# Causal masks as products in row groups, one transpose piece for rows 0 to 255, and a new order in a fused attention, experts and gated convolution kernel

## The chip, the cores and the metric

One core of a Trainium2 chip runs the whole program. The metric is the device time of one execution in microseconds; the time of a kernel is the median of its runs. The engines are TensorE (PE), VectorE (DVE), ScalarE (ACT), GpSimd (POOL) and SyncE (SP), which issues all DMAs here.

## The reference

Three layers follow one another, for 4 batch elements of 576 rows and 512 features.

```python
# 1 attention, 8 heads of 64: averaged over groups of 4 rows, plus a band |i-j| < 4
out_d   = softmax(scale * q_d @ k_d.T) @ v_d            # 144 x 144, repeated 4 times
out_loc = softmax(where(|i-j| < 4, scale * q @ k.T, -1e9)) @ v
x = out_d_repeated + out_loc
# 2 experts, 4 of them, each causal attention of 64 features; the 2 best by gate count
for e in range(4):
    s = scale * (x @ wq[e]) @ (x @ wk[e]).T
    s = where(causal, -1e9, s)                          # causal: key after query
    out += weight_e[:, None] * (softmax(s) @ (x @ wv[e]) @ wo[e])
# 3 gated convolution with 5 taps over rows
result = (sigmoid(conv5(out)) * (out @ w_val)) @ w_out
```

## The kernel before

Features lie on the partitions, rows in the columns. Most products are done as three float32r products of split operands (`mm3`, lines 1126 to 1128: high by high, low by high, high by low). The 576 rows of a batch element are taken in halves of 256 and 320 columns.

**Pieces and planner.** The program is registered as pieces: each has an engine, a cost, the buffers that it reads and writes, and a function that issues its instructions. `Plan.order` then walks simulated time with these costs and picks, engine by engine, the ready piece with the lowest due number whose buffers are free. The due numbers are a list written out in the kernel (`DUE`, one for each piece), and the engine of a piece that could run on several is a digit of another list (`PICK`). The order that comes out is the program's; at run time every engine works through its own queue in it.

**Attention** (`load_pair`, `down_path`, `band_scores`, `band_values`) runs for 4 pairs of heads of each batch element. SP loads queries, keys and values of a pair; pairs of rows are added (lines 891 and 898), the averaged scores are line 1000, the band scores line 1053 after a mask product of line 1045, the softmax lies on DVE, ACT and POOL (lines 940 to 987), its transposes are lines 1010 and 1066, the values lines 1026 and 1085, and the split result is x (lines 744 and 761).

**Projections** (`project`) turn x into values and gate logits (line 1192) and queries and keys (line 1210), each as four accumulated `mm3` products, the weights split at the start. The product of two weight matrices is line 842.

**Experts** (`experts`) come in two halves: query blocks T = 0 and 1 (rows 0 to 255), then T = 2, 3 and 4; `pr` is a pair of experts, one on partitions 0 to 63 and one on 64 to 127. `expert_scores` does the score products of both experts in row groups of 64 (line 1266) and then adds the causal mask to the diagonal block as one full-array product of an identity and `cmask` for each T and expert (line 1270). `exponentials` takes the minimum (line 1292, DVE) and the exponential (line 1300, ACT). `keys_on_rows` transposes the exponentials into two PSUM banks, one for each half of the query rows (line 1323), and copies each bank to SBUF (line 736, DVE or ACT). The weighted sum with the values is line 1426; `factors` brings the sums and gates to rows (lines 1358 to 1394); line 1432 multiplies both.

**Gated convolution** (`tail`): the product with `wo`, the taps as lines 1472 to 1486, the gate, the product with `w_val` and the last one with `w_out`, and the result's DMA (line 1524).

The next batch element's attention is registered between the experts and the tail of this one, so that their pieces can fill each other's waits.

Of the kernel before, what the change touches and what calls it, by code (L numbers as in the profile page):

```python
# [14 lines left out]
BF16 = mybir.dt.bfloat16  # L15
# [12 lines left out]
    "c_d": 5, "c_mo": 8, "c_ms": 3, "c_mt": 6, "c_o": 4, "c_s": 3, "c_t": 4, "c_w": 3, "o_00": 0, "o_01": 1,  # L28
# [255 lines left out]
class Plan:  # L284
# [64 lines left out]
    def order(self):  # L349
# [37 lines left out]
        while True:  # L387
            for e, queue in queues.items():
# [38 lines left out]
                if e == "pe":  # L427
                    if p.kind != groups:
                        cost += 0.09 if p.kind else 0.14
                        groups = p.kind  # L430
# [54 lines left out]
def f32r(n):  # L485
    return max(0.459 * n + 5, 112) / 1000
# [1097 lines left out]
```

## Time and profile before

| | us |
|---|---|
| median of 3 runs | 410.54 (410.47 to 414.11) |
| profiled execution, its own time | 409.69 |
| its span, first to last instruction | 408.0 |
| TensorE busy | 370.2 |
| VectorE busy | 317.6 |
| ScalarE busy | 253.2 |
| GpSimd busy | 192.0 |

The span is 1.7 us shorter than the profiled execution's own time, which is 0.85 us under the median of the runs. Busy times are sums over the span, and matmuls overlap in the array, so a busy TensorE need not be at its peak. The mean granted clock of TensorE is 0.937 of full speed.

### The profile page before, as it was taken

The page shows a single profiled execution, that of the slowest core. Times are in us where ns is not written, and L with a number is a line of the kernel's source. Part 1 is how long each engine was busy: PE and PEld are TensorE (multiplying, and loading weights), DVE is VectorE, ACT ScalarE, POOL GpSimd, SP SyncE. Part 2 cuts the span into 40 slices and gives each one's busy share as a digit, 9 for nine tenths or more (in the row PEclk, how much of TensorE's full clock was granted, in tenths as well). Part 3 has the DMA queues.
Part 4 walks back from the last instruction along what each step waited for, and adds up shares of the span by engine and source line. Part 5 has one row for each costly group of instructions (what it writes and reads, how often), then busy time and mean ns, then how long its engine had stood idle before and what let it go on. Part 6 is the DMA issues. An engine that isn't in the chain of part 4 may idle for free.

```text
span 408.0 us, 12119 instructions
## 1 busy us (share of the span) xinstructions
PE 370.2 (91%) x4672; PEld 317.0 (78%) x4672; DVE 317.6 (78%) x893; ACT 253.2 (62%) x879; POOL 192.0 (47%) x273
## 2 busy tenths in 40 slices
PE   1755779998888989999999999999999999999996
PEld 1444368886667777997988899988997799988896
DVE  3899579579779998799889499498977665958771
ACT  3477354377946975866648687365777456368571
POOL 7495365046537563825427357034654135224260
PEclk9965568999589999999999999999999999999999
DMA  7982445214202431421131244102120000001012
GB/s 217 247 258 65 144 123 158 67 38 124 77 31 71 103 108 38 137 73 42 42 108 41 74 134 123 55 6 69 45 91 16 2 2 2 0 34 35 2 39 79
DMA packets 26122, 31.81 MB, mean 78 GB/s; under 512 B 2384, under 2 KB 17872, under 8 KB 26064
## 3 DMA queue, kind: packets, MB, share of 16 engines
q1 hardware_dynamic: 26064, 31.03, 26.2%
q8 instruction: 37, 0.61, 0.6%
q14 instruction: 21, 0.17, 0.2%
HBM read 26.31 MB, written 4.72 MB: 76 GB/s over the span
## 4 chain that ended last, share of the span: by engine, by line
PE 66%; DVE 17%; DMA 6%; ACT 5%; issue 2%; POOL 2%; SPq 1%; ACTq 0%; POOLq 0%; DVEq 0%
PE ps L1126 14%; PE ps L1127 13%; PE ps L1128 13%; PE ps L1426 4%; PE ps L1266 3%; PE ps L1323 3%; DMA vw<-in_vx_dram 2%; PE ps L1026 2%; PE ps L1085 2%; PE ps L842 2%; PE ps L1000 2%; DMA kt<-in_kT_dram 1%; PE ps L1053 1%; ACT p L949 1%; PE ps L1066 1%
## 5 line engine op out<-in xcount | busy, mean ns | idle before, releaser
L1486 DVE SCALAR_TENSOR_TENSOR row<-ps,cw,row 128x256 f32<-128x256 f32 (+1 forms) x89 | 43.4, 509 | 7.6 <-ACT row L1472 2.7
L1300 ACT ACTIVATE pe<-ps,mmin 128x128 f32<-128x128 f32 (+4 forms) x80 | 41.5, 524 | 11.0 <-DVE mmin L1292 5.9
L949 ACT ACTIVATE p<-ps,mx 128x54 f32<-128x54 f32 (+1 forms) x120 | 40.4, 337 | 11.2 <-PE ps L1066 3.7
L1484 POOL TENSOR_TENSOR row<-row,row 128x320 f32<-128x320 f32 (+1 forms) x39 | 32.5, 841 | 23.4 <-DVE row L1486 8.7
L1292 DVE TENSOR_REDUCE mmin<-ps 128x1 f32<-128x512 f32 (+4 forms) x80 | 35.8, 474 | 7.6 <-PE ps L1270 6.6
L1126 PE MATMUL ps<-gh,wout_h 128*128 128x256 f32 (+1 forms) x128 | 39.5, 308 | 2.3 <-DVE qb L1236 1.3
L1126 PE MATMUL ps<-xh,wqk_h 128*128 128x256 f32 (+1 forms) x128 | 40.2, 314 | 0.9 <-DVE kl L761 0.9
L1128 PE MATMUL ps<-gh,wout_l 128*128 128x256 f32 (+1 forms) x128 | 37.9, 296 | 0.0
L1127 PE MATMUL ps<-gl,wout_h 128*128 128x256 f32 (+1 forms) x128 | 37.8, 295 | 0.0
L1127 PE MATMUL ps<-xl,wqk_h 128*128 128x256 f32 (+1 forms) x128 | 37.7, 295 | 0.0
L1128 PE MATMUL ps<-xh,wqk_l 128*128 128x256 f32 (+1 forms) x128 | 37.7, 295 | 0.0
L987 POOL TENSOR_TENSOR p<-p,sm 128x324 f32<-128x324 f32 (+1 forms) x29 | 23.1, 800 | 16.9 <-DVE sm L976 8.7
L1426 PE MATMUL ps<-mpT,vE 128*64 128x320 f32 (+4 forms) x224 | 27.8, 381 | 0.0
L1000 PE MATMUL ps<-kd,qd 64*64 64x144 f32 x192 | 19.0, 337 | 9.7 <-POOL kd L898 8.8
L1126 PEld LDWEIGHTS ps<-gh,wout_h 128*128 128x128 f32 x128 | 24.2, 189 | 3.5 <-DVE qb L1236 1.6
L1126 PEld LDWEIGHTS ps<-xh,wqk_h 128*128 128x128 f32 x128 | 24.1, 188 | 2.6 <-DVE kl L761 1.1
L1127 PEld LDWEIGHTS ps<-xl,wqk_h 128*128 128x128 f32 x128 | 24.2, 189 | 0.2 <-issue 0.2
L1128 PEld LDWEIGHTS ps<-gh,wout_l 128*128 128x128 f32 x128 | 24.1, 188 | 0.1
L1127 PEld LDWEIGHTS ps<-gl,wout_h 128*128 128x128 f32 x128 | 24.1, 189 | 0.0
L1126 PE MATMUL ps<-wvg_h,xh 128*128 128x260 f32 (+1 forms) x80 | 23.8, 297 | 0.4 <-DVE row L1432 0.4
L1128 PEld LDWEIGHTS ps<-xh,wqk_l 128*128 128x128 f32 x128 | 24.1, 188 | 0.0
L1426 PEld LDWEIGHTS ps<-mpT,vE 128*64 128x64 f32 (+1 forms) x224 | 14.6, 141 | 12.1 <-issue 3.9
(225 smaller groups left out, 1230.0 us busy)
## 6 DMA issues: line engine op xcount, KB each, us to landing
vw<-in_vx_dram SPq DMA_DIRECT2D x32, 162.0 KB
qt<-in_qT_dram SPq DMA_DIRECT2D x16, 288.0 KB
kt<-in_kT_dram SPq DMA_DIRECT2D x16, 288.0 KB
v<-in_vx_dram SPq DMA_DIRECT2D x16, 288.0 KB
out_dram<-o SPq DMA_DIRECT2D x16, 160.0 KB
v<-in_w_val_dram SPq DMA_DIRECT2D x4, 512.0 KB
v<-in_w_out_dram SPq DMA_DIRECT2D x4, 512.0 KB
out_dram<-o SPq DMA_DIRECT2D x16, 128.0 KB
```

The costliest lines, as they stand in the source:

```text
L949: nc.scalar.activation(pv()[:, i], sv()[:, i], AF.Exp, scale=scale, bias=mx.t[:n, i:i + 1], accum_out=sums()[:, i:i + 1])
L987: ENG[norm].tensor_mul(pv(), pv(), sm.t[:n, :g].unsqueeze(2).to_broadcast([n, g, w]))
L1000: nc.tensor.matmul(s.t[r, t * SD:(t + 1) * SD], qd.t[r, t, :], kd.t[r, :], start=True, stop=True)
L1126: nc.tensor.matmul(p, ah, bh, start=first, stop=False)
L1127: nc.tensor.matmul(p, ah, bl, start=False, stop=False)
L1128: nc.tensor.matmul(p, al, bh, start=False, stop=last)
L1266: nc.tensor.matmul(s.t[:, o:o + P * (t + 1)], a.t[r, P * t:P * t + P], z.t[r, :P * (t + 1)], start=(k == 0 and t == T[0]), stop=False)
L1292: nc.vector.tensor_reduce(out=m.t[:, a:a + 1], in_=s.t[:, o:o + n], op=ALU.min, axis=AX.X)
L1300: nc.scalar.activation(pe.t[:, c0:c1], s.t[:, o:o + c1 - c0], AF.Exp, bias=m.t[:, 0:1], scale=-1.0, accum_out=sums.t[:, a:a + 1] if last e ...
L1426: nc.tensor.matmul(av.t[64 * e:64 * e + 64, z:n], vE.t[:kr, j, 2 * pr + e, :], pT.t[:kr, e, k0:k0 + n - z], start=(j == 0), stop=(j == Tl))
L1484: nc.gpsimd.tensor_add(g.t[:, :nn], g.t[:, :nn], g2.t[:, :nn])
L1486: nc.vector.scalar_tensor_tensor(g.t[:, :nn], x2.t[:, k:k + nn], cw.t[:, m, k:k + 1], g.t[:, :nn], op0=ALU.mult, op1=ALU.add)
```

## The change

1. **Masks.** The mask of a block T was one full-array product for each expert, 128 columns. It becomes two products in row groups of 64 for each expert: rows 0 to 63 of the query block get the triangle and 64 columns of the large value (128 columns in all), rows 64 to 127 the triangle over the last 64 columns. The two experts use different row groups, and a copy of the identity with its column halves exchanged (`identx`) serves where row group and output half differ. 64 mask products become 128. The constants `cmask` and `cmask2` become one tile `causal`; `identx` is two more small copies.
2. **Rows 0 to 255.** The exponentials of T = 0 and T = 1 are written into one tile for each expert (T = 1 behind column 128) and not two. Their transposes were a piece of 4 and a piece of 8 with two PSUM banks and two copies each (128 and 256 columns); they become one piece of 12 with two banks and two copies of 384 columns. In all 8 transpose pieces and 16 copies fewer, and the same number of transposes.
3. **Order and engines.** All due numbers and engine digits are new, and so are two caps on PSUM banks: `c_d` from 5 to 6, `c_s` from 3 to 4. The planner's costs are changed at some twenty places (the issue of a DMA, float32r products, GpSimd, and others); they touch nothing but the order.

```diff
 PARAMS = {
-    "c_d": 5, "c_mo": 8, "c_ms": 3, "c_mt": 6, "c_o": 4, "c_s": 3, "c_t": 4, "c_w": 3, "o_00": 0, "o_01": 1,
+    "c_d": 6, "c_mo": 8, "c_ms": 3, "c_mt": 6, "c_o": 4, "c_s": 4, "c_t": 4, "c_w": 3, "o_00": 0, "o_01": 1,
...
 def f32r(n):
-    return max(0.459 * n + 5, 112) / 1000
+    return max(0.4533 * n + 2.4, 112) / 1000
...
+            nc.vector.tensor_copy(identx[:, 0:64], ident[:, 64:128])
+            nc.vector.tensor_copy(identx[:, 64:128], ident[:, 0:64])
...
-            nc.gpsimd.memset(cmask, 0.0)
-            nc.gpsimd.affine_select(out=cmask, in_=cmask, compare_op=ALU.is_ge, fill=BIG, base=0,
-                                    pattern=[[-1, P]], channel_multiplier=1)
-            nc.gpsimd.memset(cmask2, 0.0)
+            nc.gpsimd.memset(causal[:, 0:64], 0.0)
+            nc.gpsimd.memset(causal[:, 64:P], BIG)
...
                 for t, o in zip(T, at):
-                    for s in ss:
-                        nc.tensor.matmul(s.t[:, o + P * t:o + P * t + P], identb, cmask, start=False, stop=(t == T[-1]))
+                    for u, d in enumerate((o + P * t, o + P * t + 64)):
+                        for e, s in enumerate(ss):
+                            r = slice(64 * e, 64 * e + 64)
+                            nc.tensor.matmul(s.t[:, d:o + P * t + P], (identb if u == e else identx)[r], causal[r, 0:P - 64 * u],
+                                             start=False, stop=(t == T[-1] and u == 1))
...
+            if Ts == (0, 1):
+                blocks, c, w, o = (2, 0, 1), 0, P, 0
+            else:
+                blocks, o = tuple(range(T, -1, -1)), off
+                c = base - T * w
+                if c < 0:
+                    c, o = c + off, 0
+            nf, pts = len(blocks), [bank("mt"), bank("mt")]
+
+            @piece("pe", 0.066 * 2 * nf, pes, pts + [(pT, "%dt" % T)], kind="row")
+            def _():
+                for e, pe in enumerate(pes):
+                    for k, j in enumerate(blocks):
+                        for u, pt in enumerate(pts):
+                            r, i = slice(64 * u, 64 * u + 64), (nf * e + k) * 64
+                            nc.tensor.transpose(pt.t[:, i:i + 64], pe.t[r, j * P:(j + 1) * P], ident[r, r])
...
-                    pes = {}
+                    pes = [buf("pe") for _ in range(2 if Ts[0] < NTOK - 1 else 1)]
                     for T, e, sp in expert_scores(y, pr, Ts):
-                        pes.setdefault(T, []).append(exponentials(T, e, sp, es if T == NTOK - 1 else rs))
-                    for T in Ts:
-                        keys_on_rows(b, pr, T, pes[T], pT, base, w, P * (T - T0))
+                        exponentials(T, e, sp, es if T == NTOK - 1 else rs, pes[e], P if Ts == (0, 1) and T else 0)
+                    keys_on_rows(b, pr, Ts, pes, pT, base, w, P * (Ts[-1] - T0))
```

What the two lists of due numbers say, put in ascending order, of TensorE's pieces around the first experts (batch element 0, `pr` = 0, from their scores of T = 0 and 1 to the transposes of these):

```
old: scores pr0 T0,1 | 5 attention pieces of element 1 (lines 1053, 1066, 1026, 1000, 1085), scores pr1 T0,1 | transposes T0
new: scores pr0 T0,1 | 12 query and key products of element 0's second half (columns 256 to 575), 7 attention pieces
     of element 1, scores pr1 T0,1, scores pr0 T2 | transposes T0,1
```

In the old list those 12 products all stand before the first scores. By the same reading the piece behind a masked score piece is, in the new list, one in row groups 14 times of 24 (lines 1010, 1066 and 1323), one in another division of the array 7 times and a full-array one 3 times. SP's first loads, by the same reading: old, queries of pair 0 (288 KB), part of `w_val` (512 KB), keys of pair 0 (288 KB); new, part of `wqk` (256 KB), part of `w_val` (512 KB), keys of pair 0 (288 KB), part of `wo` transposed (128 KB), queries of pair 0 (288 KB). Of the 129 digits that place work of element 0's attention and of the query, key, value and `w_val` weights, 57 name DVE in the old list and 44 in the new one, 29 and 36 ACT, 38 and 44 POOL; 5 and 5 name a form without that step.

## Rows read from the trace of the kernel before

**Rows 1.** The page, parts 1 and 2: TensorE's line, and the clock in 40 slices.

```profile
PE 370.2 (91%) x4672; PEld 317.0 (78%) x4672; DVE 317.6 (78%) x893; ACT 253.2 (62%) x879; POOL 192.0 (47%) x273
...
PEclk9965568999589999999999999999999999999999
```

**Rows 2.** Windows by stage: length, busy us of each engine (instructions), granted clock, DMA share, GB/s.

```profile
0.00:8.80 8.80, 0.00 (x0) 0.00 (x0) 2.35 (x12) 3.79 (x10) 7.16 (x33) 1.00 0.75 224
8.80:23.70 14.90, 11.48 (x213) 7.55 (x214) 12.96 (x34) 7.61 (x35) 7.56 (x9) 1.00 0.92 239
23.70:57.70 34.00, 24.12 (x379) 17.59 (x378) 26.42 (x65) 19.77 (x81) 20.21 (x29) 0.50 0.49 141
57.70:64.70 7.00, 5.04 (x122) 4.03 (x120) 6.43 (x18) 5.39 (x24) 4.22 (x5) 0.75 0.58 179
64.70:100.00 35.30, 34.40 (x435) 29.68 (x436) 27.76 (x82) 18.79 (x74) 14.81 (x19) 1.00 0.32 87
100.00:102.10 2.10, 0.54 (x21) 0.31 (x12) 2.00 (x9) 1.87 (x10) 0.86 (x3) 1.00 0.18 42
102.10:115.80 13.70, 12.50 (x84) 8.93 (x84) 9.42 (x33) 9.12 (x42) 5.42 (x9) 0.50 0.19 57
115.80:194.00 78.20, 71.75 (x892) 61.36 (x891) 71.48 (x190) 55.39 (x188) 44.25 (x53) 1.00 0.27 79
194.00:398.00 204.00, 203.59 (x2510) 181.07 (x2507) 157.50 (x455) 129.69 (x419) 86.68 (x119) 1.00 0.15 46
398.00:408.00 10.00, 6.75 (x46) 6.44 (x44) 1.25 (x3) 1.77 (x4) 0.86 (x1) 1.00 0.21 75
```

**Rows 3.** TensorE's timeline, 92 to 107: start, length, instruction, idle before and its releaser.

```profile
91.92 0.31 PE L1127 MATMUL ps<-xl,wqk_h 128*128 128x320 f32 x1
...
92.50 0.31 PE L1128 MATMUL ps<-xh,wqk_l 128*128 128x320 f32 x1
...
93.96 0.47 PE L1266 MATMUL ps<-kh,qh 64*128 64x128 f32 x4
...
99.32 0.91 PE L1085 MATMUL ps<-pT,vw 54*64 54x48 f32 x48
101.79 0.34 PE L1323 MATMUL ps<-ident,pe 64*128 64x64 f32 x4 [1.56 <-DVE row L1101]
103.06 0.69 PE L1323 MATMUL ps<-ident,pe 64*128 64x64 f32 x8 [0.93 <-DVE mpT L736]
```

**Rows 4.** Windows, 2 to 8 us: the rate of the first loads.

```profile
2.00:8.00 6.00, 0.00 (x0) 0.00 (x0) 1.93 (x6) 1.79 (x7) 5.26 (x24) 1.00 0.91 292
```

**Rows 5.** TensorE's timeline, 271 to 274: masks of T = 0 and 1, then transposes.

```profile
272.08 0.45 PE L1266 MATMUL ps<-kl,qh 64*128 64x128 f32 x4
272.31 0.45 PE L1266 MATMUL ps<-kh,ql 64*128 64x128 f32 x4
272.68 0.40 PE L1270 MATMUL ps<-cmask,identb 128*128 128x128 bf16 x4
273.01 0.46 PE L1323 MATMUL ps<-ident,pe 64*128 64x64 f32 x8
273.40 0.83 PE L1000 MATMUL ps<-kd,qd 64*64 64x144 f32 x10
```

**Rows 6.** TensorE's timeline, 337 to 339.2: masks followed by a full-array product.

```profile
338.12 0.39 PE L1266 MATMUL ps<-kh,ql 64*128 64x128 f32 x4
338.44 0.40 PE L1270 MATMUL ps<-cmask,identb 128*128 128x128 bf16 x4
338.65 0.37 PE L1126 MATMUL ps<-wvg_h,xh 128*128 128x260 f32 x1
```

**Rows 7.** Groups by line and shape, DVE: the copies of transposed exponentials (busy, mean ns).

```profile
L736 DVE COPY mpT<-ps 128x384 f32<-128x384 f32 x7 | 3.8, 551 | 0.9 <-PE ps L1323 0.9
...
L736 DVE COPY mpT<-ps 128x256 f32<-128x256 f32 x8 | 3.3, 417 | 0.3 <-PE ps L1323 0.2
...
L736 DVE COPY mpT<-ps 128x128 f32<-128x128 f32 x8 | 2.2, 276 | 0.0
```

More of the change, by code (lines that the diff above doesn't have):

```diff
@@ L428, in order @@
                     if p.kind != groups:
-                        cost += 0.09 if p.kind else 0.14
+                        cost += 0.1
                         groups = p.kind
@@ L497, in gps @@
 def gps(n, k=1):
-    return 0.15 * k + 0.0021 * n + 0.08 * (k - 1)
+    return 0.13 + 0.00185 * n
 def moved(rows, size, queues=16):
@@ L678, in late_constants @@
     def late_constants():
-        @piece("dve", 0.15, [], [late], after=[eye], kind="port")
+        @piece("dve", 0.4, [], [late], after=[eye], kind="port")
         def _():
             nc.vector.tensor_tensor(fold, ident[:, 0:64], ident[:, 64:128], op=ALU.add)
+            nc.vector.tensor_copy(identx[:, 0:64], ident[:, 64:128])
+            nc.vector.tensor_copy(identx[:, 64:128], ident[:, 0:64])
         @piece("pool", 2.0, [], [late])
         def _():
-            nc.gpsimd.memset(cmask, 0.0)
-            nc.gpsimd.affine_select(out=cmask, in_=cmask, compare_op=ALU.is_ge, fill=BIG, base=0,
-                                    pattern=[[-1, P]], channel_multiplier=1)
-            nc.gpsimd.memset(cmask2, 0.0)
+            nc.gpsimd.memset(causal[:, 0:64], 0.0)
+            nc.gpsimd.memset(causal[:, 64:P], BIG)
             for h in range(2):
-                m = cmask2[64 * h:64 * h + 64, :]
+                m = causal[64 * h:64 * h + 64, 0:64]
                 nc.gpsimd.affine_select(out=m, in_=m, compare_op=ALU.is_ge, fill=BIG, base=0,
@@ L729, in cost, with whole @@
         return vec(n, k, k - 1) if eng == "dve" else gps(n, k)
+    def whole(eng, n, src):
+        return 0.13 + 0.0009 * n if eng == "pool" else cost(eng, n, src)
     def copy(eng, n, out, src, reads, writes):
@@ L740, in split @@
         eh = pick(name + "h", "act", "dve", "pool") if inside else pick(name + "h", "act", "dve")
-        @piece(eh, cost(eh, n, read), [read], [wh], kind=port(eh) if inside else None)
+        @piece(eh, whole(eh, n, read), [read], [wh], kind=port(eh) if inside else None)
         def _(src=src):
@@ L775, in chunk @@
         if src.dtype != mybir.dt.int64:
-            @piece("sp", 0.65, [], [f], delay=moved(P, 4 * n), kind="dma")
+            @piece("sp", 0.5, [], [f], delay=moved(P, 4 * n), kind="dma")
             def _():
@@ L787, in part @@
             return (a0, a1)[k].t[:, :n].bitcast(I32)
-        @piece("sp", 0.65, [], [raw], delay=moved(P, 8 * n), kind="dma")
+        @piece("sp", 0.5, [], [raw], delay=moved(P, 8 * n), kind="dma")
         def _():
@@ L794, in whole @@
             return f.t[:, :n].bitcast(I32)
-        @piece("act", act(n, True), [raw], [a1])
+        @piece("act", act(n, True) + 0.03, [raw], [a1])
         def _():
@@ L861, in load_pair @@
         qt, kt, v4, vw = buf("qt"), buf("kt"), buf("v4"), buf("vw")
-        @piece("sp", 0.65, [], [qt], delay=moved(P, 4 * S), kind="dma")
+        @piece("sp", 0.5, [], [qt], delay=moved(P, 4 * S), kind="dma")
         def _():
             nc.sync.dma_start(out=qt.t, in_=qT[b, hp])
-        @piece("sp", 0.65, [], [kt], delay=moved(P, 4 * S), after=ends, kind="dma")
+        @piece("sp", 0.5, [], [kt], delay=moved(P, 4 * S), after=ends, kind="dma")
         def _():
             nc.sync.dma_start(out=kt.t[:, KB], in_=kT[b, hp])
-        @piece("sp", 0.65, [], [v4], delay=moved(144, 2048, 12), kind="dma")
+        @piece("sp", 0.5, [], [v4], delay=moved(144, 2048, 12), kind="dma")
         def _():
@@ L876, in load_pair @@
         for h in range(NR):
-            @piece("sp", 0.65, [], [vw], delay=moved(WK * 2 * NC, 4 * P), kind="dma")
+            @piece("sp", 0.5, [], [vw], delay=moved(WK * 2 * NC, 4 * P), kind="dma")
             def _(h=h):
@@ L978, in softmax @@
         norm = pick("n_" + key, "act", "dve", "pool")
-        @piece(norm, g * (act(w, True) + 0.09) if norm == "act" else cost(norm, g * w) - 0.08 * (norm == "pool"),
+        @piece(norm, g * (act(w, True) + 0.09) if norm == "act" else cost(norm, g * w),
                [p, sm], [p], kind=port(norm))
@@ L993, in down_path @@
         s = bank("s")
-        @piece("pe", 0.735, [qd, kd], [s], kind="quad")
+        @piece("pe", 0.66, [qd, kd], [s], kind="quad")
         def _():
@@ L1038, in band_scores @@
         ss = [bank("s"), bank("s")]
-        @piece("pe", 1.0, [qt, kt], ss, after=[edges, eyeb], kind="quad")
+        @piece("pe", 0.74, [qt, kt], ss, after=[edges, eyeb], kind="quad")
         def _():
@@ L1058, in band_values @@
         vw, pTs, pts = ld[2], [buf("pT"), buf("pT")], [bank("t"), bank("t")]
-        @piece("pe", 0.36, ps, pts, after=down + blanks, kind="row")
+        @piece("pe", 0.41, ps, pts, after=down + blanks, kind="row")
         def _():
@@ L1075, in band_values @@
         pos = [bank("o"), bank("o")]
-        @piece("pe", 0.62, [vw] + pTs, pos, after=down, kind="quad")
+        @piece("pe", 0.735, [vw] + pTs, pos, after=down, kind="quad")
         def _():
@@ L1133, in gates @@
         sh = [P, NTOK, E, E]
-        @piece("dve", 1.9, [L], [ge, gw, gm], kind="port")
+        @piece("dve", 1.63, [L], [ge, gw, gm], kind="port")
         def _():
@@ L1152, in _ @@
             nc.scalar.activation(gw.t[:, 0], gw.t[:, 0], AF.Exp)
-        @piece("dve", 1.2, [gw, gm], [gw, gm], kind="port")
+        @piece("dve", 0.95, [gw, gm], [gw, gm], kind="port")
         def _():
@@ L1256, in expert_scores @@
             at = [sum(P * (u + 1) for u in T[:k]) for k in range(len(T))]
-            @piece("pe", sum(3 * f32r(P * (t + 1)) + 0.16 for t in T), [(qh, (mine,)), (ql, (mine,)), (kh, half), (kl, half)], ss,
+            @piece("pe", sum(3 * f32r(P * (t + 1)) + 0.15 for t in T), [(qh, (mine,)), (ql, (mine,)), (kh, half), (kl, half)], ss,
                    kind="row")
@@ L1280, in _, with exponentials @@
                 if c1 == S:
-                    nc.tensor.matmul(s.t[:, h - 64:h], identb, cmask2, start=False, stop=True)
+                    nc.tensor.matmul(s.t[:, h - 64:h], identb, causal[:, 0:64], start=False, stop=True)
             sp.append((s, 0, c0, c1))
         return [(T[0], 0, sp)]
-    def exponentials(T, e, sp, sums):
+    def exponentials(T, e, sp, sums, pe, off):
         last = T == NTOK - 1
-        pe, m = buf("pe"), buf("mmin")
+        m = buf("mmin")
         for a, (s, o, c0, c1) in enumerate(sp):
@@ L1312, in place @@
             return pT.t[:, :, c:c + nf * w].rearrange("p e (j q) -> p e j q", q=w)[:, :, :, a:a + n]
-        if T < NTOK - 1:
-            pts = [bank("mt"), bank("mt")]
-            @piece("pe", 0.058 * 2 * nf, pes, pts + [(pT, "%dt" % T)], kind="row")
-            def _():
-                for e, pe in enumerate(pes):
-                    for j in range(nf):
-                        for u, pt in enumerate(pts):
-                            r, i = slice(64 * u, 64 * u + 64), (nf * e + nf - 1 - j) * 64
-                            nc.tensor.transpose(pt.t[:, i:i + 64], pe.t[r, j * P:(j + 1) * P], ident[r, r])
-            for u, pt in enumerate(pts):
-                copy(pick("mp_%d%d%d%d" % (b, pr, T, u), "act", "dve"), P * nf, lambda u=u: place(o + 64 * u, 64),
-                     lambda pt=pt: pt.t[:, :nf * P].rearrange("p (e j q) -> p e j q", e=2, q=64), [pt], [(pT, "%d%d" % (T, u))])
-            return
         pe, pt, pt2 = pes[0], bank("mt"), bank("mt")
@@ L1520, in _ @@
                 nc.vector.tensor_scalar_mul(o.t[:, :nn], p.t[:, :nn], 0.5)
-        @piece("sp", 0.65, [o], [], delay=moved(P, 4 * nn), kind="dma")
+        @piece("sp", 0.5, [o], [], delay=moved(P, 4 * nn), kind="dma")
         def _():
```

40 lines of the change are left out of this document (23 added, 17 removed), and 416 rows, old and new, of the table DUE.

## Prediction

> **What bounds the kernel now.** I read the page's first two parts, then windows cut where the clock or TensorE's load changes, then TensorE's timeline at the one place in the middle where it stands still, and last the timelines around the masks. TensorE is busy 91% of the span [rows 1], and the windows show that this is two regimes [rows 2]. From 194 to 398 us it is busy 203.59 of 204.00 us at full clock: there only less TensorE work makes the kernel shorter. Before 194 it waits, and the clock falls. In the first 8.8 us it does nothing. From 8.8 to 64.7 it is idle for 14.9 - 11.48 = 3.4, 34.0 - 24.12 = 9.9 and 7.0 - 5.04 = 2.0 us, with the clock at half (1.2 GHz, 0.50 in the column) from 23.7 to 57.7 and for half of the next 7 us. VectorE is busy there for 12.96 + 26.42 + 6.43 = 45.8 of 55.9 us, more than the other two elementwise engines. A second fall is at 102.1 to 115.8. In between and after it are small holes: 0.9 us in 64.7 to 100, 6.45 in 115.8 to 194. What an edit is worth is therefore a question of where its work stands.
>
> **The stall at 100 us, the largest term.** The scores of the first pair of experts start at 93.96, their first transposes at 101.79 and the second ones at 103.06 [rows 3]: minimum, exponential and their queues take 7.8 and 9.1 us. TensorE's other work ends with the band values that start at 99.32, and it waits 1.56 and 0.93 us. After this wait the clock is at half until 115.8. The loss in numbers [rows 2]: 2.10 - 0.54 = 1.6 us idle, 13.70 - 12.50 = 1.2 us idle, and 12.50 us of busy time at half clock of which half, 6.25 us, would not have been needed. Sum 9.0. In the new order twelve query and key products stand between these scores and the transposes. Each is three matmuls of 320 columns that start (92.50 - 91.92) / 4 = 0.145 us apart [rows 3], so 12 x 3 x 0.145 = 5.2 us. The scores and the pieces that filled the gap before took 99.32 + 0.91 - 93.96 = 6.3 us, and they are all still there. 11.5 us of work against a chain of 9.1 us (the later of the two, since one piece now waits for all four exponentials): covered, with 2.4 us to spare. Behind the transposes of T = 0 nothing waits that the wait for T = 1 could hold up, because the weighted sum needs both. I take the whole 9.0; the range of this term is 0 to 9.0. Next late after it is the chain from the transposes over their copies, the weighted sum and line 1432 to the tail; the new list also places products of the next batch element there.
>
> **The head.** Against the change: in the new order the queries of pair 0 come behind 256 + 512 + 288 + 128 KB, so that both operands are there after 1472 KB and not after 1088. At the 292 GB/s of the first loads [rows 4] the 384 KB are 1.3 us, at a place where TensorE and the engines behind it have nothing else. For it: 13 of 57 pieces leave VectorE for ScalarE and GpSimd in this part. At the 0.42 us of a 256-column operation [rows 7] that is 5.4 of its 45.8 busy us; VectorE is busy for 82% of the stretch, so not all of it comes back, and I take 60%, 3.3 us. Sum -2. Bounds: +2 (the loads come late and VectorE was not what was waited for) and -7 (all 5.4, and 1.6 more since some of the half-clock work meets a full clock).
>
> **Small holes.** 7.4 us are idle in 64.7 to 100 and 115.8 to 194 at full clock [rows 2]. VectorE is busy for 71.48 of 78.2 us in the second stretch, so an order cannot fill all of it. With 16 PSUM copies fewer, each pair of copies of 128 and 256 columns becoming one of 384, VectorE or ScalarE wins 276 + 417 - 551 = 142 ns each time [rows 7], 2.3 us in all and 0 in the saturated part, where it is hidden beside TensorE. I take -5, between 0 and -7.4.
>
> **The masks on TensorE.** Four full-array masks (T = 0 and 1, two experts) take 338.65 - 338.44 = 0.21 us [rows 6], 53 ns each, 0.107 a T. In row groups the two experts can run side by side: 128 + 64 columns, at best 0.08 a T. The nearest row for what they do in row groups is the transposes, also with 64 rows of weights, 128 columns of them and few moving columns: 8 in 273.40 - 273.01 = 0.39 us [rows 5], 49 ns each, so four take 0.196. Stream: -0.027 to +0.089 a T, times 32 blocks -0.9 to +2.8. Then the changes of the array's division. Low-by-high scores take 0.23 when the same division follows (272.08 to 272.31) and 0.37 when the masks follow (272.31 to 272.68), so 0.14 is the change; the masks there take 0.33 until the transposes, against 0.21 where a full-array product follows: another 0.12 [rows 5, 6]. A piece followed by another in row groups saves both, one followed by a full-array product saves none, since the change only moves behind the masks. 24 pieces: 0 to -6.2, together -7.1 to +2.8. In the new list 14 of the 24 are followed by a piece in row groups, 7 by one in another division (which save the first change only) and 3 by a full-array one: 14 x 0.26 + 7 x 0.14 = 4.6 us, against the middle of the stream's range, +0.95. I take -3.5.
>
> The Trainium skill speaks against this part: "TensorE: Matmul & The Clock Gate", section "LDWEIGHTS (loading the stationary operand)", says that a weight load takes its time by the columns of the weights, not by the rows. By that, 64-row loads are as long as the old ones and there are twice as many, so that the stream stands at its worse end: +2.8 - 4.6 = -1.8 in place of -3.5, and the whole sum 1.7 us higher. No row of before shows 64-row bf16 loads.
>
> **The merged transposes** are the same 12 instructions; 8 pieces fewer save at most 8 x 0.14 us of division changes [rows 5]. I take -0.5.
>
> **The sum.** Stall -9, head -2, holes -5, masks -3.5, transposes -0.5: -20 from the profiled 409.7 gives 389.7. The median of the runs is 0.85 above the profiled execution, so 390.5. The edits proper are worth 4 of this; the rest is the order.
>
> **Rivals.**
> *The wait moves.* VectorE is 91% busy in 115.8 to 194 [rows 2]; if it delivers late there, what is gained at 100 us is in part given back as new waits without a fall of the clock. Half of the stall (4.5), half of the holes (2.5), and 4 of edits: -11, 399.5. For it: VectorE keeps almost as much work. Against it: the twelve products stand where the wait was.
> *The head leaves the half clock early.* If the rebalanced pieces keep TensorE fed from about 43 us on, 14 of the 34 half-clock us, with 14/34 x 24.12 = 9.9 us of busy time, would run at full clock: 5.0 less, and 3 of the idle time with it, 382.5. For it: a work shift away from VectorE. Against it: 9.9 us of idle time in 34.
> *The order doesn't do on the chip what its list says.* The planner's costs are not the chip's; the old order too was planned without the stall that it shows. If a comparable stall comes back, the holes stay and the head is no better, only the edits' 4 us or less remain: 406.5 to 411.
> *Slower: the merged transposes stop the queue.* TensorE works its queue in order, and the merged piece waits for four exponentials, which came 1.27 us after the first two [rows 3]. Where fillers run out, TensorE stands still as at 100 us. One such place cost 9.0. [...] If it happens for both pairs of element 0 and one of element 1, 27 us are lost where 9 were, less 11 of the other terms: about 418. Against it: after 194 us the list has no lack of fillers.
>
> Not a rival, but a bound: after 194 us nothing but TensorE work counts, so a gain over 28 us would need most of the head's losses too.
>
> **Chances.** Forecast 0.55, the wait moves 0.20, the head at full clock 0.12, no effect 0.08, slower 0.05. A measurement of this kernel tells about 1% from no change, 4.1 us. Faster by more: 0.55 + 0.20 + 0.12 = 0.87; within: 0.08; slower: 0.05. The range should hold the forecast, the wait that moves and most of the early full clock: 381 (the early full clock, with 1.5 more of the masks' better end) to 404 (the wait that moves, with the masks at -1.8 and 2.8 more of the head's worse end).
>
> **What will show it.** Right: between the first scores and transposes of the experts TensorE has no idle time, and the clock has one half-clock stretch in the head and none around 100 us; the saturated stretch begins some 16 us earlier; the masks of T = 0 and 1 start 0.23 us after the last scores and not 0.37. Wrong would make it: a second fall of the clock anywhere behind the head, a first averaged-scores product later than 11 us, or VectorE waits of several us in the second batch element. If the saturated stretch became longer than 204 us by more than 2 us without more work in it, the masks in row groups are dearer than both ends of my bound.

## The result and the profile after

The changed kernel takes 393.68 us in the median of 4 runs (392.45 to 394.8) against 410.50 us for the kernel before (4 runs, 409.57 to 414.11): a ratio of 0.9583, 95% interval 0.9521 to 0.9644, some 17 us less. The prediction was 390.5 (381 to 404). Of the signs that it named, some came and some did not: the stall at 100 us is gone and the masks start sooner, but there are falls of the clock behind the head, at 177.7 and at 331.3, the first averaged-scores product comes at 11.30 us and not before 11, and the saturated stretch begins 9.5 us earlier and not 16. Such a fall and so late a first product it had named as signs of being wrong. The profiled execution took 392.88 us with a span of 391.2.

The page of the kernel after, parts 1 and 2, TensorE's line and the granted clock in 40 slices, answers to [rows 1]:

```profile
PE 355.4 (91%) x4736; PEld 312.7 (80%) x4736; DVE 322.5 (82%) x871; ACT 244.8 (63%) x868; POOL 206.7 (53%) x302
...
PEclk9978599999999999996999999999999999899999
```

Windows of the kernel after, cut where its own clock or load changes, answer to [rows 2]; columns as there:

```profile
0.00:11.30 11.30, 0.00 (x0) 0.03 (x1) 6.26 (x20) 4.48 (x11) 7.99 (x33) 1.00 0.82 256
11.30:24.02 12.72, 10.17 (x177) 6.90 (x181) 10.75 (x26) 8.43 (x39) 6.42 (x10) 1.00 0.92 254
24.02:30.90 6.88, 6.80 (x140) 5.45 (x128) 6.47 (x16) 6.19 (x24) 5.29 (x8) 0.50 0.79 209
30.90:37.70 6.80, 3.26 (x120) 2.89 (x120) 6.53 (x19) 6.00 (x31) 6.72 (x10) 1.00 0.59 154
37.70:48.00 10.30, 8.18 (x149) 6.95 (x150) 9.40 (x21) 7.38 (x31) 7.27 (x10) 0.50 0.57 168
48.00:58.00 10.00, 7.25 (x157) 4.76 (x156) 7.66 (x24) 5.60 (x25) 6.20 (x11) 1.00 0.55 156
58.00:174.00 116.00, 111.37 (x1542) 96.34 (x1541) 107.35 (x297) 79.63 (x279) 77.02 (x101) 1.00 0.33 93
174.00:177.60 3.60, 0.89 (x25) 0.75 (x24) 3.57 (x3) 2.49 (x10) 3.39 (x6) 1.00 0.47 114
177.60:184.50 6.90, 6.09 (x84) 5.13 (x86) 5.34 (x16) 2.23 (x10) 3.84 (x5) 0.51 0.11 27
184.50:194.00 9.50, 9.50 (x152) 8.70 (x146) 7.05 (x18) 6.57 (x32) 6.62 (x9) 1.00 0.48 143
194.00:381.00 187.00, 184.86 (x2190) 168.03 (x2185) 148.11 (x414) 113.96 (x378) 75.13 (x106) 0.99 0.11 35
381.00:391.20 10.20, 7.00 (x48) 6.74 (x46) 4.05 (x9) 1.81 (x4) 0.82 (x1) 1.00 0.18 64
```

Every microsecond of a span is one of three things: TensorE idle (length minus busy), lost to half clock (busy time that full clock would have saved, half of the busy time at 0.50), or work at full clock. I summed windows of 1 us over the whole span. Before: 37.8 idle, 20.1 half clock, 350.1 work. After: 35.8, 12.1 and 343.3. So the 16.8 us between the two spans are 2.0 of idle time, 8.0 of clock and 6.8 of work. The idle time, which the forecast wanted to shorten most, is almost the same in size and lies elsewhere:

- The head (0 to 64.7 before, 0 to 58 after): idle 24.1 and 22.3, half clock 13.8 and 7.5. It is 8.1 better, though the first product comes at 11.30 and not at 8.8.
- The stall at 100 us: gone, all 9.0. From the first scores (80.31) to the first transposes (94.64) TensorE is idle for 0.65 us, at full clock.
- Other idle time up to 194: 7.4 before, 4.6 after.
- New: 174.0 to 184.5, with 2.7 + 0.8 idle and 3.0 lost to half clock, 6.5 together. TensorE's list of waits says `PE ps L1266 <- DVE row L1509: 3.5, 1, 3.5`.
- The saturated part: 0.4 idle before, 2.1 idle and 1.6 of half clock after (a wait of 1.6 us that ends at 330.6, and the fall of the clock behind it).

What ended the stall at 100 us in the kernel before is named by [rows 3] itself: VectorE's line 1101, and then VectorE's copy of the first transposes. The same stretch in the timelines of ScalarE and VectorE:

```profile
98.27 0.51 ACT L1300 ACTIVATE pe<-ps,mmin 128x256 f32<-128x256 f32 x1
98.64 0.23 ACT L1300 ACTIVATION_READ_ACCUMULATOR pe<-ps,mmin 128x1 f32 x1
...
98.91 1.18 DVE L1358 TENSOR_SCALAR rs<-rs 128x4 f32<-128x4 f32 x1
...
101.29 0.44 DVE L1101 TENSOR_TENSOR row<-ps,od 128x288 f32<-128x288 f32 x1
...
102.73 0.28 DVE L736 COPY mpT<-ps 128x128 f32<-128x128 f32 x1
```

The last of the four exponentials that the transposes read is through at 98.87, 4.9 us after the scores' start and 1.4 us before TensorE's other work ends (99.32 + 0.91 = 100.23). Lines 1101 and 736 read PSUM: TensorE stood still until VectorE had emptied banks for the transposes, and not for the exponentials.

What VectorE and GpSimd do at the new stall, from their timelines in the kernel after:

```profile
173.13 0.19 DVE L976 RECIPROCAL sm<-sm 128x6 f32<-128x6 f32 x1
173.67 3.75 DVE L1371 TENSOR_SCALAR rs<-rs 128x4 f32<-128x4 f32 x1 [0.35 <-ACT pe L1303]
177.45 0.18 DVE L1375 RECIPROCAL rs<-rs 128x4 f32<-128x4 f32 x1
177.88 0.48 DVE L1509 SCALAR_TENSOR_TENSOR row<-row,ps 128x320 f32<-128x320 f32 x1
...
173.58 0.70 POOL L1101 TENSOR_TENSOR row<-row,od 128x288 f32<-128x288 f32 x1
174.23 0.84 POOL L744 CAST gh<-row 128x320 fp32r<-128x320 f32 x2
175.03 0.72 POOL L987 TENSOR_TENSOR p<-p,sm 128x324 f32<-128x324 f32 x1
175.72 1.67 POOL L761 TENSOR_TENSOR gl<-row,gh 128x320 fp32r<-128x320 f32 x2
177.78 0.61 POOL L1382 TENSOR_TENSOR row<-rs,gw 128x256 f32<-128x256 f32 x1 [0.38 <-DVE rs L1375]
```

Line 1371 adds 1e-9 to four row sums. It takes 0.17 us as a rule and 3.75 here. It begins in the middle of a GpSimd instruction, GpSimd goes on for six instructions without a gap, and the addition ends 0.03 us after the last of them (175.72 + 1.67 = 177.39; 173.67 + 3.75 = 177.42). Behind it in VectorE's queue stands line 1509, which frees the PSUM bank that TensorE waits for. The same addition is in the kernel before, where it took 1.18 us at 98.9, just ahead of the stall there (line 1358 above).

The masks, in TensorE's timeline of the kernel after, answer to [rows 5]:

```profile
80.64 0.39 PE L1266 MATMUL ps<-kl,qh 64*128 64x128 f32 x4
80.87 0.39 PE L1266 MATMUL ps<-kh,ql 64*128 64x128 f32 x4
81.11 0.23 PE L1272 MATMUL ps<-causal,identx 64*128 64x128 bf16 x1
81.11 0.23 PE L1272 MATMUL ps<-causal,identb 64*128 64x128 bf16 x1
...
81.26 0.19 PE L1272 MATMUL ps<-causal,identb 64*128 64x64 bf16 x1
81.29 0.50 PE L1010 MATMUL ps<-ident,p 64*72 64x64 f32 x12
81.72 0.41 PE L1126 MATMUL ps<-xh,wqk_h 128*128 128x320 f32 x1
```

The masks start 0.24 us after the last scores (0.37 before), eight products take 81.29 - 81.11 = 0.18 us, and the piece behind them begins at once. The two experts' products start together.

### The profile page after: what moved, and what is told of

Same layout as the page of the kernel before. It is cut to its first block, busy times and chain, and to the rows that moved or that the text cites. A ratio compares the mean times of both kernels' runs of the same rounds, so it can differ in the third digit from the quotient of the medians.

```text
span 391.2 us, 12232 instructions
## 1 busy us (share of the span) xinstructions
PE 355.4 (91%) x4736; PEld 312.7 (80%) x4736; DVE 322.5 (82%) x871; ACT 244.8 (63%) x868; POOL 206.7 (53%) x302
## 5 line engine op out<-in xcount | busy, mean ns | idle before, releaser
L1496 POOL TENSOR_TENSOR row<-row,row 128x320 f32<-128x320 f32 (+1 forms) x44 | 36.6, 836 | 35.4 <-DVE row L1498 13.9
L1498 DVE SCALAR_TENSOR_TENSOR row<-ps,cw,row 128x256 f32<-128x256 f32 (+1 forms) x84 | 41.8, 510 | 10.4 <-POOL row L1496 6.3
L1303 ACT ACTIVATE pe<-ps,mmin 128x256 f32<-128x256 f32 (+4 forms) x80 | 41.4, 525 | 13.1 <-DVE mmin L1295 9.7
L949 ACT ACTIVATE p<-ps,mx 128x54 f32<-128x54 f32 (+1 forms) x114 | 38.5, 339 | 3.7 <-PE ps L1066 0.4
L1295 DVE TENSOR_REDUCE mmin<-ps 128x1 f32<-128x256 f32 (+4 forms) x80 | 35.3, 473 | 5.2 <-PE ps L1272 2.5
L1128 PE MATMUL ps<-xh,wqk_l 128*128 128x256 f32 (+1 forms) x128 | 37.8, 295 | 0.0
L1127 PE MATMUL ps<-xl,wqk_h 128*128 128x256 f32 (+1 forms) x128 | 37.8, 295 | 0.0
L1000 PE MATMUL ps<-kd,qd 64*64 64x144 f32 x192 | 17.4, 317 | 12.7 <-DVE kd L898 11.3
L987 POOL TENSOR_TENSOR p<-p,sm 128x324 f32<-128x324 f32 (+1 forms) x23 | 18.9, 826 | 13.2 <-DVE sm L976 8.8
L1491 ACT ACTIVATE row<-ps,cw 128x320 f32<-128x320 f32 (+1 forms) x44 | 21.2, 503 | 5.4 <-POOL row L1496 3.7
L1127 PEld LDWEIGHTS ps<-xl,wqk_h 128*128 128x128 f32 x128 | 24.1, 188 | 0.2 <-issue 0.2
L761 POOL TENSOR_TENSOR gl<-row,gh 128x320 fp32r<-128x320 f32 (+1 forms) x20 | 16.9, 853 | 13.8 <-ACT gh L744 10.2
L1000 PEld LDWEIGHTS ps<-kd,qd 64*64 64x64 f32 x192 | 13.0, 149 | 13.8 <-issue 12.6
```

The lines of the kernel that those rows point to most:

```text
L949: nc.scalar.activation(pv()[:, i], sv()[:, i], AF.Exp, scale=scale, bias=mx.t[:n, i:i + 1], accum_out=sums()[:, i:i + 1])
L987: ENG[norm].tensor_mul(pv(), pv(), sm.t[:n, :g].unsqueeze(2).to_broadcast([n, g, w]))
L1000: nc.tensor.matmul(s.t[r, t * SD:(t + 1) * SD], qd.t[r, t, :], kd.t[r, :], start=True, stop=True)
L1127: nc.tensor.matmul(p, ah, bl, start=False, stop=False)
L1128: nc.tensor.matmul(p, al, bh, start=False, stop=last)
L1295: nc.vector.tensor_reduce(out=m.t[:, a:a + 1], in_=s.t[:, o:o + n], op=ALU.min, axis=AX.X)
```

## The experiments

Each ratio is to runs of the kernel before that stand beside those of the kernel in question; their medians are 409.3 to 410.9 us, so differences between medians of two experiments are good to a microsecond or two.

**1 and 2. Without the addition, in both kernels.** Line 1371 (1358 before) is left out, so that the four row sums lack 1e-9.

```diff
-            nc.vector.tensor_scalar_add(rs.t, rs.t, EPS)
+            pass
```

The changed kernel without it: 

> Leaves out the addition of 1e-9 to the experts' sums (16 instructions of 4 columns on VectorE); the order of all else is that of the changed kernel. Theory one, that the wait at 174 us is this one instruction, which lasted 3.75 us while GpSimd ran without a gap: the idle time there and the fall of the clock go, 6 us, so about 387.5. Rival, that the instruction only stands where a chain of exponentials, gates and tail waits anyway: within 1.5 us of 393.7.

The kernel before without it: 

> The kernel before without the same addition. If the stall at 100 us came in part from the 1.18 us that this instruction took at 98.9 us, its idle time shrinks by about 1 us and the clock may stay up: 402 to 409. If the stall is a matter of the order alone: 410 to 411, with a fall of the clock at 102 us as before.

The changed kernel without it took 390.45 us (389.01 to 392.04), ratio 0.9523 (0.9472 to 0.9573). TensorE is busy for 3.60 of 3.60 us from 174.0 and the clock stays up. Some of the idle time moved on, as VectorE's and GpSimd's timelines of that kernel show:

```profile
175.34 2.37 DVE L908 TENSOR_TENSOR v<-v 72x512 f32<-72x512 f32 x1 [0.23 <-DMA v<-in_vx_dram]
179.14 2.05 DVE L915 TENSOR_TENSOR vd<-v 72x256 f32<-72x256 f32 x1
...
175.46 1.71 POOL L761 TENSOR_TENSOR gl<-row,gh 128x320 fp32r<-128x320 f32 x2
177.10 1.08 POOL L1382 TENSOR_TENSOR row<-rs,gw 128x256 f32<-128x256 f32 x1
178.13 0.44 POOL L744 CAST gh<-row 128x320 fp32r<-128x320 f32 x1
```

Lines 908 and 915 take 0.67 and 0.41 us where they are shortest. Now they are the ones that stand beside GpSimd's run, and TensorE waits 0.9 and 1.6 us further on. The addition was the first VectorE instruction to meet the run, not the only one. The kernel before without it took 408.5 us (405.74 to 409.18), ratio 0.9945 (0.9915 to 0.9974): about 2 us, and its clock falls behind 100 us as before. In its profiled execution the stall is no smaller: from 98 to 118 us, 4.3 us idle and 4.7 lost to half clock, against 3.0 and 6.2 with the addition. TensorE waits there for the same two VectorE lines, 0.77 us for 1101 (1.56 before) and 1.37 us for the copy (0.93 before). So the addition did not make that stall; where the 2 us come from is not shown.

**3 and 4. The masks alone.** The changed kernel with full-array masks, and the kernel before with masks in row groups; two constants go with them, all else stays.

```diff
-                    for u, d in enumerate((o + P * t, o + P * t + 64)):
-                        for e, s in enumerate(ss):
...
+                    for s in ss:
+                        nc.tensor.matmul(s.t[:, o + P * t:o + P * t + P], identb, cmask, start=False, stop=(t == T[-1]))
```

New order, old masks: 

> The changed kernel with the old full-array masks of 128 columns, in the new order (two more constants on GpSimd at the start). If the row groups win the changes of division, as the forecast had it, 3.5 us; the trace after has 6 us less TensorE work than before, so if all of that is the masks, 399. Rival, by the rule that weight loads of 64 rows are no shorter and there are twice as many: 1.7 us or less, 395.5 or under.

Old order, new masks: 

> The kernel before with only its masks as products in row groups, old order, old transposes. Theory: 3.5 to 5.5 us less, 405 to 407, since the saturated stretch from 194 us holds half of the masks and the rest meets stretches with idle time, perhaps only half of it: 407.5. Rival: within 1 us of 410.5.

The new order with old masks took 398.32 us (397.78 to 401.09), 4.6 more than with the new masks; TensorE's busy time is 358.7 against 355.4. The rest of the 4.6 is not TensorE's work: the first product comes 0.4 us later (at 11.73) and there is 1.6 us more idle time in all. The old order with new masks took 407.87 us, ratio 0.9968 (0.9931 to 1.0006), which is not told from none by itself; TensorE's busy time fell from 370.2 to 366.9, by the same 3.3. Counted along TensorE's timelines, the array's division changes 227 times before and 192 times with the new masks alone, 209 times in the new order with old masks and 173 times with the new ones: the masks take away some 35 changes in either order. At the 0.12 to 0.14 us of [rows 5, 6] that would be 4.2 to 4.9 us; the 3.3 us of busy time are less than 0.1 us a change, so those two places were dearer than the average.

**5. Both edits in the old order.** The kernel before with masks in row groups and merged transposes, with its old due numbers, digits and costs (without those of the pieces that no longer exist). The order is near the old one, not the same: some 780 of VectorE's 887 instructions stand in the old sequence.

> The kernel before with both edits proper, masks in row groups and merged transposes of rows 0 to 255, in the old kernel's due times, digits and costs, so that the order is as near the old one as the missing pieces allow. Theory (the edits themselves are worth 2 to 4.5 us, all the rest of the 16.8 us is the order): 406 to 408.5 us, with TensorE idle in front of the transposes near 100 us as before. Rival (the edits need no new order; they remove the wait at 100 us themselves): 397 to 401 us. Rival (merged transposes cost, since eight row blocks wait for the last of four exponentials): 410.5 us or more.

It took 414.19 us (413.01 to 416.07), ratio 1.0108 (1.0057 to 1.016): slower than the kernel before, as the third of the theories said, and 6 us above the new masks alone. Its list of TensorE's waits has a releaser that the kernel before doesn't have at all, the exponentials:

```profile
PE ps L1080 <- ACT pe L1257: 1.7, 2, 1.2
...
PE ps L1279 <- ACT pe L1257: 0.9, 1, 0.9
```

(Lines are 46 less here: 1279 is the transposes, 1257 the exponential.) That is 2.6 us of new waits that end with an exponential, in front of products and of the merged transposes; idle time in all is 42.2 against 39.4 with the masks alone. The other 3 us of the profiled spans are work at full clock, 350.0 against 346.8. I did not find which instructions got longer; the changes of division (197 against 192) are too few for it.

**6 and 7. The head's engines.** 129 copies and roundings belong to the head; 66 of them have another engine in the new kernel. Old engines in the new kernel, and new engines in the old one:

```diff
 PICK = (
-    (digits of the head, new)
+    (digits of the head, old)
```

New order, old engines: 

> The changed kernel with the old choice of engine for the 129 copies and roundings of the head (66 of them differ); all else, the due times too, is the changed kernel's. Theory (the head is 8 us shorter because VectorE, ScalarE and GpSimd share its copies in another way): the projections start later than at 58 us, 397 to 400 us. Rival (the order of the pieces did it, not the engines): 393 to 395 us.

Old order, new engines: 

> The kernel before with the changed kernel's choice of engine for the 129 copies and roundings of the head (66 of them differ); due times and all else are the old kernel's. Theory (the engines of these copies are what shortens the head, by themselves): 401 to 404 us, half clock in the head for 17 to 25 us in place of 37. Rival (engines and order fit only each other, as the changed kernel with the old engines suggests with its loss of 10 us, more than the whole gain of the head): 408 to 414 us.

The first took 404.12 us (401.66 to 405.23), ratio 0.9844: 10.4 more than the changed kernel. The second took 416.48 us (412.92 to 418.32), ratio 1.0157 (1.0115 to 1.0199): 6 more than the kernel before. Each order is worse with the other's engines. The page's clock line, first of the new order with old engines:

```profile
PEclk9966586999999999998599999999999999999999
```

and of the old order with new engines:

```profile
PEclk9965777999698999999999999999999999999999
```

In the old order with the new engines there is less half clock in this one execution (slices 4 to 7 read 5777 where they were 5568 [rows 1], and half clock costs 16.3 us in the whole span in place of 20.1), but TensorE is idle for 44.4 us in place of 37.8. So the gain is not the rebalancing of engines alone, as I had it, and not the order alone. Nor is all of the 10.4 us the head's: TensorE has done by 64.6 us with the old engines what it has done by 58.0 in the changed kernel (work counted at full clock), 6.6 later, and the rest is lost behind it, where the clock falls from 189.6 to 199.9.

**8. The order of the first loads.** SyncE's first five loads in the changed kernel: queries of pair 0 first, one block of weights later.

```diff
+    at = [i for i, p in enumerate(order) if p.engine == "sp"][:5]
+    first = [order[i] for i in at]
+    for i, k in zip(at, (4, 1, 2, 0, 3)):
+        order[i] = first[k]
```

> The changed kernel, in which SyncE's first five loads stand in another order: queries of pair 0, the weights of the values, keys of pair 0, and only then the two other weights. Nothing else is moved. Theory (the first product, at 11.3 us, waits for VectorE's averaged keys, and these for the load of the keys behind the weights): the first product starts 1.3 to 2.5 us sooner; 391.5 to 393 us. Rival (in the head VectorE's queue is what decides, or the early weights do): the first product comes as late as before or what stands behind it waits for the weights; 393.7 us or more.

It took 395.79 us (393.84 to 396.69), ratio 0.9644, and the first product came at 14.53 us and not at 11.30. VectorE's timeline of this kernel:

```profile
8.91 0.76 DVE L761 TENSOR_TENSOR wqk_l<-o,wqk_h 128x512 fp32r<-128x512 f32 x1 [1.54 <-ACT wqk_h L744]
11.21 0.69 DVE L811 SCALAR_TENSOR_TENSOR o<-o,o 128x512 f32<-128x512 f32 x1 [1.54 <-ACT o L806]
14.08 0.30 DVE L898 TENSOR_TENSOR kd<-row 128x144 f32<-128x144 f32 x1
```

In the changed kernel these three start at 6.51, 7.74 and 10.86. The averaged keys (line 898) stand in VectorE's queue behind the roundings of the weights, so the load that I put back was the one that the first product waited for. Moving the operands of the first product to the front made it 3.2 us later.

**9 to 12. The wait at 174 us.** Four ways at it. In 9, three roundings of weights at 173 us go from GpSimd to ScalarE (`g011`, `g012`, `g013`). In 10, the addition takes 1e-9 from a column in SBUF. 11 is both. 12 is 9 with that one addition of the sixteen on ScalarE.

```diff
-            (nc.scalar.copy if eh == "act" else ENG[eh].tensor_copy)(hi(), src())
+            (nc.scalar.copy if eh == "act" or name in ("g011", "g012", "g013") else ENG[eh].tensor_copy)(hi(), src())
...
-            nc.vector.tensor_scalar_add(rs.t, rs.t, EPS)
+            nc.vector.tensor_scalar(rs.t, rs.t, tiny[:, 0:1], None, op0=ALU.add)
...
+            adds.append(0)
+            if len(adds) == 5:
+                nc.scalar.activation(rs.t, rs.t, AF.Copy, bias=EPS)
+            else:
+                nc.vector.tensor_scalar_add(rs.t, rs.t, EPS)
```

9: 

> The changed kernel, in which the first rounding of three weight pieces (the ones that GpSimd does from 173 us on, in a burst of seven instructions with no gap) is done by ScalarE at the same place of the order. The addition of 1e-9 stays on VectorE. Theory (VectorE's addition to the row sums waits as long as GpSimd goes on without a gap): the addition at 173.7 us lasts about 1 us or less in place of 3.75, TensorE's wait at 174 us shrinks from 3.5 to under 1 us, and the clock doesn't fall there; 388 to 391 us. Rival (the addition is long for a reason of its own, such as its source or a semaphore): it lasts 3 us or more again, and the time stays at 393.7.

10: 

> The changed kernel, in which the addition of 1e-9 to the row sums takes 1e-9 from a column of 128 numbers in SBUF and not from the instruction; engine, place and operands are otherwise the same. A near relative of this form, the addition to one column per row, took 204 ns at most in the changed kernel, also in the middle of GpSimd instructions, while the addition to four columns ended with GpSimd in every place where both met. Theory (VectorE's form that needs the access it shares with GpSimd is what waits): the addition at 174 us lasts 0.2 us, TensorE's wait of 3.5 us is gone, and the next VectorE instructions with two inputs from SBUF wait instead, as they did without the addition; 389 to 391 us. Rival (one column, and not the source of the number, made the relative short): it lasts 3 us or more again, 393.7 us.

11: 

> The kernel with the number from a column, and in addition the three roundings of weights at 173 us on ScalarE in place of GpSimd, so that GpSimd's run without a gap is shorter when VectorE's next instructions with two inputs from SBUF come. Theory: both waits get smaller, 387 to 390 us, the fastest of all. Rival (ScalarE's exponentials come later by the three roundings, 1.3 us, and TensorE waits for them): no better than with the column alone.

12: 

> The changed kernel with the three roundings of weights at 173 us on ScalarE in place of GpSimd, and with the one addition of 1e-9 that meets GpSimd's run there, the fifth of sixteen, on ScalarE too, behind the exponentials whose sums it takes; the other fifteen stay on VectorE, and all is computed. Theory (it is VectorE's access beside GpSimd, not the addition): the reciprocal follows the addition within 0.3 us, TensorE's wait of 2.7 to 3.5 us at 174 us is gone, VectorE's next instructions with two inputs from SBUF wait less than the 2.4 and 2.1 us that they waited without the addition, and TensorE's clock doesn't fall there; 388 to 391 us. Rival (ScalarE, with three roundings and the addition more, brings its exponentials later): TensorE waits 1.5 us or more for ScalarE within the next 10 us, 391 to 394 us.

9 took 393.58 us (390.58 to 395.4). The addition lasted 2.97 us and not the 1 that I expected, because the other GpSimd instructions only moved up: its run now ends at 174.91 + 1.68 = 176.59, and the addition at 173.66 + 2.97 = 176.63. My number was wrong, while the addition's end moved with the end of the run. 10 took 393.93 us (390.88 to 395.59), and the rival was right:

```profile
L1373 DVE TENSOR_SCALAR rs<-rs,tiny x16: 214/229/3749, 88.9 to 363.4; 128x4 f32<-128x4 f32 x16
```

(least, median and longest of 16, in ns.) Where the number comes from plays no part. The other addition of 1e-9, to one column, stayed at or under 216 ns in all eight places in this kernel too. It differs in its single column, and in adding two numbers in one instruction; which of the two keeps it short is not shown. 11 took 392.43 us (391.38 to 394.38): the addition waits 2.96 us, as in 9.

12 took 389.85 us (387.32 to 391.41), ratio 0.953 (0.9477 to 0.9583), the fastest of all. Its VectorE timeline:

```profile
174.82 0.18 DVE L1380 RECIPROCAL rs<-rs 128x4 f32<-128x4 f32 x1 [0.59 <-ACT rs L1374]
174.92 0.41 DVE L1537 TENSOR_SCALAR o<-ps 128x256 f32<-128x256 f32 x1
...
176.37 1.73 DVE L909 TENSOR_TENSOR v<-v 72x512 f32<-72x512 f32 x1
...
179.54 1.66 DVE L916 TENSOR_TENSOR vd<-v 72x256 f32<-72x256 f32 x1
```

and its windows where the changed kernel stood still:

```profile
174.00:177.60 3.60, 3.60 (x70) 3.19 (x70) 2.98 (x8) 3.54 (x17) 3.60 (x7) 1.00 0.72 197
177.60:184.50 6.90, 5.68 (x141) 4.68 (x137) 6.85 (x20) 4.50 (x17) 5.56 (x8) 1.00 0.33 85
```

The wait of 3.5 us and the fall of the clock are gone; of the rival, 1.1 us of waiting for an exponential is there. 12 and 9 differ by one instruction's engine and by 3.7 us between their medians, 2.7 us by their ratios to the kernel before, whose intervals overlap. The runs of 12 all lie below those of the changed kernel (392.45 to 394.8), while the intervals of the two ratios overlap.

## Why the prediction was right, point by point

**The stall at 100 us, -9.0.** Right in size, wrong in mechanism. "Minimum, exponential and their queues take 7.8 and 9.1 us" takes the time until the transposes start for the time until the exponentials are there. These were through after 4.9 us, which the old fillers of 6.3 us already covered; the last 2.9 us of the 7.8 before the first transposes, and all of the second wait, were VectorE's late emptying of PSUM banks, as the releasers in [rows 3] say. So the sum "11.5 us of work against a chain of 9.1 us" answers a wait that was not there. The twelve query and key products do follow the first scores (from 81.72 on), there is 0.65 us of idle time up to the transposes and no fall of the clock between 58 and 177.7; but no run moves the twelve products alone, so which part of the new order did it (the products, the two caps on PSUM banks, VectorE's own new sequence) stays open. That the term came out at its full 9.0 is luck as far as the reasoning goes.

**The head, -2.** Undersized: -8.1. The sentence "13 of 57 pieces leave VectorE ... I take 60%, 3.3 us" is the step that failed. It priced the head by VectorE's work alone and gave the clock no term of its own but 1.6 us in a bound: 6.3 of the 8.1 us are clock, 17.2 us of half clock in place of some 37.5. What came is the rival of the head that leaves the half clock early, which I had given 0.12 and 8 us. The loads were costed rightly in direction (first product 2.5 us later), with the wrong cause: by experiment 8 it is the weights' load that decides, through VectorE's queue. Experiments 6 and 7 say that engines and order made the rest together. The 8.1 is one pair of executions: kernel 9, whose head is the changed kernel's instruction for instruction, has done as much TensorE work by 60.1 us, kernel 12 by 60.7, and the kernel before without the addition, with the old head, 2 us later than the kernel before. So the gain is 5 us or more in each of these executions, above the forecast, and 8.1 is not its middle.

**Small holes, -5.** Wrong in sign. The old holes did shrink, 7.4 to 4.6, but a new stall of 6.5 stands at 174, and the saturated part lost 3.3. The step ended at "VectorE is busy for 71.48 of 78.2 us", a share. Which instruction waits for what cannot be read from a share, and the rival of the wait that moves came in this place, with a fall of the clock that I had excluded for it.

**The masks, -3.5.** Right in mechanism and in sum: 3.3 us of TensorE's busy time in either order, 4.6 us of the kernel in the new one by experiment 3, with 35 changes of division fewer. The stream costs 0.18 us for eight products (T = 0 and 1), near the 0.16 of my best end and far from 0.39 of the transposes' row. By an estimate from 0.18 against the 0.21 of [rows 6], 16 times over, the stream gave -0.5 where I had taken +0.95, which leaves some 2.8 us for the changes of division where I had taken 4.6: the two misses cancel. Of the rule in "TensorE: Matmul & The Clock Gate", section "LDWEIGHTS (loading the stationary operand)", of the Trainium skill, the trace agrees with what it says of the rows: 95 ns in the median for 64 rows, 98 ns for 128 rows before. It does not agree on the columns: the 64-row bf16 loads of the band masks (line 1045), which stand in the trace before too, have 64 columns and not 128 and take 103 ns. The sum that I made from the section, -1.8, doesn't hold, since the loads of the two experts' row groups go side by side (81.10 and 81.10 us, 0.09 each, in the kernel after).

**The merged transposes, -0.5.** Not settled in the new order. In the old order they go with 6 us on the wrong side (experiment 5). This may be the rival "the merged transposes stop the queue" in small: 2.6 us of waits that end with an exponential are shown, the rest is not explained. In the new kernel no wait for `pe` is in TensorE's list.

**The sum.** 16.8 us between the profiled spans against 20 forecast: the stall -9.0 as forecast, the head 6.1 better, TensorE's work 2.8 better (-6.8 where masks and transposes were to give -4), and the holes with the new stall and the saturated part 12.1 worse (-2.7 + 6.5 + 3.3 where -5 was forecast). The total was near because errors of 9 and 12 us had opposite signs, and that is luck. "The edits proper are worth 4 of this; the rest is the order" is sharper than that: without their order the edits cost some 4 us (ratio 1.0108).

## What to carry to other kernels

Read a wait by what ended it, as the profile names it, before pricing what should fill it: here the named engine was VectorE and the chain that was priced had ended long before. Price the head by where its half clock ends, and by the queue in front of its first operand, and not by the busy share of one engine. Wherever GpSimd gets more work, look for VectorE instructions that read only SBUF beside its longest run without a gap, however small they are: moving GpSimd work away gave nothing by itself (393.58 against 393.68 us), and moving one such instruction of 0.17 us to ScalarE on top of it gave some 3 us. An edit that joins several waits into one belongs together with an order that hides the later of them: price it in both orders.

## What was not expected of the hardware

- A VectorE instruction of 128x4 numbers, 0.17 us alone, waited for six GpSimd instructions in a row, 3.75 us. "SBUF — State Buffer", section "SBUF: two separate sides", of the Trainium skill says that GpSimd and certain forms of VectorE instruction share a pair of ports as an exclusive lock, held by whichever starts first for a whole instruction. The trace agrees: wherever the addition was long it ended 0.02 to 0.03 us after a GpSimd instruction (it took 0.35 to 0.73 us at 126.6, 186.5, 197.8, 275.9 and 309.6). What these runs add is that VectorE can be passed over at the turn from one GpSimd instruction to the next, five times in a row at 174 us. At 187.0 and 276.3 it was let in at such a turn; what decides that stays open.
- The addition to one column never waited: 204 ns in the median and 215 at most, also at 107.1, in the middle of a GpSimd instruction of 1.29 us.
- The head's clock is not the same in all executions. With the same instructions there, but for one constant that is set, 24.0 to 58.0 us ran at half clock for 17.2 us in the changed kernel; in kernel 10 the windows there read 0.64, 0.86, 0.50 and 0.84 where the changed kernel has 0.50, 1.00, 0.50 and 1.00, and half clock costs 16.0 us over its span against 12.1. The same wait of 1.6 us near 330 us is followed by a fall of the clock in the changed kernel and in kernels 1 and 11, and by none in 9, 10 and 12. Differences of 2 to 4 us between two single executions can be that alone.
